# Seven products for part of the input stage of a fused attention and squared-ReLU kernel on one Trainium2 core

## The chip, the cores and the metric

The kernel runs on one core of one Trainium2 chip. The metric is the device time of one execution in microseconds; the kernel before has a median of 283.25 us over three runs (282.54 to 285.18). PE is TensorE, DVE VectorE, ACT ScalarE, POOL GpSimd, and SP the engine that issues most DMAs.

## The reference

Attention in chunks of 64 tokens is followed by a feed-forward layer with a squared ReLU. Scores and values stay within a chunk, so attention is small; the two products with w_in (512 x 2048) and w_out (2048 x 512) over 4608 tokens are nearly all of the arithmetic.

```python
scores = scale * np.matmul(q_c, k_c.transpose(0, 1, 2, 4, 3))   # chunks of 64 x 64
attn = np.exp(scores - max); attn = attn / (sum(attn) + 1e-09)
out = np.matmul(attn, v_c)
x = out.transpose(0, 2, 1, 3).reshape(B * S, H * D)             # 4608 x 512
h = np.maximum(x @ w_in, 0.0)
return (h * h @ w_out).astype(np.float32)
```

## The kernel before, in words

The 4608 tokens are 18 groups of 256, taken two at a time as 9 blocks (0 to 8) of 512 tokens. The groups of block 7 are put together from the last 64 tokens of each batch entry (`is_whole` is false for them); all others are contiguous.

Each block has an input stage and an output stage. The input stage (`ffn_in`, L455) takes the 16 tiles of 128 of d_ff one after the other, in the order 8 to 15, then 0 to 7: four matmuls of 512 columns into one PSUM bank (L480), a relu by ACT into `rl` (L471), and a square into `gT`, by ACT for tiles 10, 14 and 3 (L473) and else by DVE (L475). The output stage (`ffn_out`, L498; block 0 has a plain one) multiplies `gT` by w_out in seven products of quarters (Strassen's scheme in Winograd's manner of saving sums), 16 matmuls of 256 columns each (L533). Two chains of PSUM, n and m, hold sums that go on accumulating from product to product while ACT and DVE read partial sums from them (L580 to L616). DVE makes five differences of quarters of `gT` for it (`difference`, L510, recorded at L493).

The order of all work is written out by hand (`manual_schedule`): each engine runs its instructions in the order in which the program issues them. Both stages are generators that yield after each d_ff tile or each half of a product; a yield is a slot. Before the next slot the main loop (L700 to L780) issues at most one piece of a DMA load, then what the plan has for this slot, then stores that were put off (`late`). The plan of block j makes attention for block j+1: SC (scores, L355: 32 small matmuls and an exp by ACT, L385), AV (values, L387: two halves, each 16 small matmuls into a tile of `ps_att`, then on DVE a reciprocal, L408, and a multiplication, L409), and XT, a transposing DMA on SP that makes `xT` (L422); and for block j+2 casts of q and k on ACT (C, L333 and L340) and transposing DMAs (TD, L351). The usual slots are in L745: SC (4, 4), AV (7, 11), XT (10, 14), C (18, 22), TD (20, 24); other slots stand beside it for block 3 and for block 6, whose next block is not whole.

PSUM has 8 banks: four for `ps_ffn` and two tiles of two banks for `ps_att` (L64, L65). `rl` has three buffers, the input pool of q and k five. POOL casts weights and early q and k, in the first three blocks; after that it has nothing but the stores of the last block (L568).

Of the kernel before, what the change touches and what calls it, by code (L numbers as in the profile page):

```python
# [10 lines left out]
FP32 = mybir.dt.float32  # L11
BF16 = mybir.dt.bfloat16
AF = mybir.ActivationFunctionType
ALU = mybir.AluOpType
# [3 lines left out]
def kernel(  # L18
# [9 lines left out]
    nc = tc.nc  # L28

    B, H, S, D = q.shape  # L30
# [27 lines left out]
    const_pool = ctx.enter_context(tc.tile_pool(name="const", bufs=1))  # L58
    w_pool = ctx.enter_context(tc.tile_pool(name="w", bufs=1))
    wst_pool = ctx.enter_context(tc.tile_pool(name="wst", bufs=5))  # L60
    in_pool = ctx.enter_context(tc.tile_pool(name="qk", bufs=5))
    att_pool = ctx.enter_context(tc.tile_pool(name="att", bufs=3))
    ffn_pool = ctx.enter_context(tc.tile_pool(name="ffn", bufs=1))
    ps_ffn = ctx.enter_context(tc.tile_pool(name="ps_ffn", bufs=4, space=bass.MemoryType.PSUM))  # L64
    ps_att = ctx.enter_context(tc.tile_pool(name="ps_att", bufs=2, space=bass.MemoryType.PSUM))  # L65

    ctx.enter_context(tc.manual_schedule())

# [5 lines left out]
    w_in_bf = w_pool.tile([128, n_dt, d_ff], BF16, name="w_in_bf")  # L74
    w_out_bf = w_pool.tile([128, n_ft, d_model], BF16, name="w_out_bf")
    w_sum = w_pool.tile([128, 3, n_ft // 2, d_model // 2], BF16, name="w_sum")

    NV = 5
    NO = 2 * NV + 1
# [7 lines left out]
    qk = {}  # L87
# [299 lines left out]
    def values(g, tiles=(0, 1)):  # L387
        e = state["e", g]
        veb = v_even[g % NV].bitcast(BF16)
        vob = [v_odd[odd_tile[g, c] % NO].bitcast(BF16) for c in range(4)]  # L390
        if 0 in tiles:
            state["x", g] = att_pool.tile([128, 2, n_hp, 2, D], BF16, name="x", bufs=3)
        x = state["x", g]
        for t in tiles:
            ps = ps_att.tile([128, 2, 512], FP32, name="ps_att")
            for hp in range(n_hp):
                for a in range(2):
                    for p in range(2):
                        c = p ^ a
                        vb = vob[2 * t + p] if a else veb[:, t]  # L400
                        nc.tensor.matmul(  # L401
                            out=ps[64 * p:64 * p + 64, a, hp * (D + 1):(hp + 1) * (D + 1)],
                            lhsT=e[64 * c:64 * c + 64, a, hp, t, :],
                            rhs=vb[64 * c:64 * c + 64, hp, 1::2],
                            start=True, stop=True)
            o = ps[:, :, 0:n_hp * (D + 1)].rearrange("p a (h d) -> p a h d", d=D + 1)
            rec = att_pool.tile([128, 2, n_hp], FP32, name="rec", bufs=4)
            nc.vector.reciprocal(out=rec, in_=o[:, :, :, D])  # L408
            nc.vector.tensor_tensor(  # L409
                out=x[:, t].rearrange("p h a d -> p a h d"),  # L410
                in0=o[:, :, :, 0:D],
                in1=rec.to_broadcast([128, 2, n_hp, D]),
                op=ALU.mult)
# [21 lines left out]
    C, CQ, CK, TD = cast_qk, cast_q, cast_k, transpose_qk_dma  # L435
    SC, AV, XT = scores, values, transpose_x

    def TA(g):
        transpose_qk(g, ps_att, ps_att)

# [8 lines left out]

    gTs = {}  # L450
    LATE_STORES = {j: 26 if j == 2 else 20 for j in range(2, len(blocks) - 1)}
    late = []
    FT_ORDER = [*range(n_ft // 2, n_ft), *range(n_ft // 2)]

    def ffn_in(j, parts, begun={}):  # L455
        if j not in gTs:
            gTs[j] = ffn_pool.tile([128, n_ft, BT], BF16, name="gT")
        gT, xT = gTs[j], xTs[j]
        for u, (c, n, ft) in enumerate((c, n, ft) for c, n, fts in parts for ft in fts):
            h = begun.get(ft)  # L460
            if h is None:
                h = ps_ffn.tile([128, 512], FP32, name="ps_ffn")
            for dt in range(n_dt // 2 if ft in begun else 0, n_dt):
                ffn_in_step(h, xT, c, n, ft, dt)
            if j < 3:
                if n == 512 or u % 2 == 0:
                    rl_tile = ffn_pool.tile([128, 512], FP32, name="rl", bufs=3).bitcast(BF16)
                rl = rl_tile[:, u % 2 * 512:] if n < 512 else rl_tile
            else:
                rl = ffn_pool.tile([128, 512], FP32, name="rl", bufs=3)  # L470
            nc.scalar.activation(out=rl[:, 0:n], in_=h[:, 0:n], func=AF.Relu)  # L471
            if (n == 512 and ft in SQUARES_ON_ACT) or (n < 512 and ft in (12, 3)):
                nc.scalar.activation(out=gT[:, ft, c:c + n], in_=rl[:, 0:n], func=AF.Square)  # L473
            else:
                nc.vector.tensor_tensor(  # L475
                    out=gT[:, ft, c:c + n], in0=rl[:, 0:n], in1=rl[:, 0:n], op=ALU.mult)
            yield
# [14 lines left out]
    def add(engine, out, in0, in1, op=ALU.add):  # L492
        engine.tensor_tensor(out=out, in0=in0, in1=in1, op=op)  # L493
# [4 lines left out]
    def ffn_out(j):  # L498
# [28 lines left out]
        def product(name, a, b, first):  # L527
            if first:
                state["chain", name] = chain(name)
            outs = state["chain", name]  # L530
            for t in range(n_tt):
                for i in range(HF):
                    nc.tensor.matmul(  # L533
                        out=outs[t],
                        lhsT=a[:, i, t * 128:(t + 1) * 128],
                        rhs=b[:, i, :],
                        start=(first and i == 0 and (last or t == 0)), stop=(i == HF - 1),
                        skip_group_check=True)
                yield
# [69 lines left out]
        for ps, cols, t in parts("m"):  # L609
            add(nc.vector, c22[:, cols], ps, s[:, cols])  # L610
            store(nc.gpsimd, c22, 1, HD, t)
        yield from product("n", d7, b21_p_b22, False)
        c11 = o_tile()
        for ps, cols, t in parts("n"):
# [96 lines left out]
    for j, grps in enumerate(blocks):  # L711
# [4 lines left out]
        def at(slot, f, g):  # L716
            plan.setdefault(slot, []).append((f, g))
# [25 lines left out]
        else:  # L743
# [3 lines left out]
                slots.update({SC: (8, 8), AV: (10, 14), XT: (13, 17)})  # L747
                go_slots = [*range(6), *range(13, 32)]
            if not is_whole(nxt[0] if nxt else 0):
                slots.update({SC: (7, 7), AV: (9, 13), XT: (12, 16)})  # L750
            if j == 2:
                loads = itertools.chain(*map(v_pieces, nxt), loads)
                slots = {SC: (8, 10), AV: (12, 15), XT: (15, 18), C: (20, 23), TD: (22, 25)}
                go_slots = [*range(16), *range(25, 36)]
            for f in (SC, AV, XT):
                for i, g in enumerate(nxt):
                    at(slots[f][i], f, g)
            if j > 2 and far and is_whole(far[0]):
                for slot, f, i in ((16, CQ, 0), (18, CK, 0), (18, TD, 0), (18, CQ, 1),
                                   (19, CK, 1), (19, TD, 1)):  # L760
                    at(slot, f, far[i])
            else:
                for f in (C, TD):
                    for i, g in enumerate(far):
                        at(slots[f][i], f, g)
            phases = [ffn_in(j, [(0, BT, FT_ORDER)]), ffn_out(j)]
        slot = 0
        for phase in phases:
            for _ in phase:
# [43 lines left out]
```

## Time and profile before

| what | before |
|---|---|
| median of three runs | 283.25 us |
| the profiled execution's own time | 281.17 us |
| its span, first to last instruction | 279.4 us |
| input stage of block 4, 5, 6, 7, 8 | 15.79, 15.55, 15.81, 15.55, 13.81 us |
| output stage of block 4, 5, 6, 7 | 12.23, 12.23, 12.45, 12.23 us |
| POOL busy from block 3 to the end | 2.91 us |

The stages are read from the chain of waits: the chain runs along PE there, and each stage begins where its first matmul does. In the table of stretches each row is one stage: its length, then each engine's busy time with the number of instructions, the granted clock of TensorE, the DMA share. In the order of time, a row gives start, length, engine, line, operation, out<-in and shapes; a row with x2 or more is several instructions of one kind in a row, and what stands in brackets is the idle time ahead of it and what ended that. Matmul ends are modelled in the profile, so the mean spacing of many is a better measure of one than its own duration.

### The profile page before, as it was taken

Reading aid. Unit: us, or ns where it says so; the run is one execution under the profiler, and the core shown is the slowest. Engines: PE = TensorE matmul, PEld = TensorE weight load, DVE = VectorE, ACT = ScalarE, POOL = GpSimd, SP = SyncE. Lnnn points to the kernel's source line nnn. Section 1 sums busy time; section 2 is a strip of 40 time slices with the busy share of each in tenths; the row PEclk is TensorE's granted clock in tenths of the full one; section 3 lists DMA queues with packets and bytes.
Section 4 is the critical chain, followed back from the end, with each engine's and each line's share of the span. In section 5 each row is a group of like instructions: output and inputs, shape, how many; then the busy total and the mean of one; then the engine's idle time right before and its main releaser. Section 6 shows DMA issues by size and latency. Waiting matters only on the chain.

```text
span 279.4 us, 7179 instructions
## 1 busy us (share of the span) xinstructions
PE 269.2 (96%) x2960; PEld 176.2 (63%) x2963; DVE 186.5 (67%) x304; ACT 160.5 (57%) x269; POOL 35.8 (13%) x62
## 2 busy tenths in 40 slices
PE   6789999989999999999999999999999999999994
PEld 4544455878774487448744874487448744874584
DVE  1446414998943595579549954995579649955793
ACT  2537615885348862877197719762877197218710
POOL 2037844240171000000000000000000000000012
PEclk9999999999999999999999999999999999999998
DMA  7999999989999999979999999979699964141003
GB/s 236 220 345 358 364 332 240 326 212 194 255 207 244 238 213 191 258 183 198 218 245 260 187 184 298 191 158 185 196 238 208 212 199 40 39 109 44 0 21 131
DMA packets 144384, 57.09 MB, mean 204 GB/s; under 512 B 110624, under 2 KB 141600, under 8 KB 144352
## 3 DMA queue, kind: packets, MB, share of 16 engines
q1 hardware_dynamic: 143296, 53.62, 83.8%
q0 software_dynamic: 912, 2.88, 2.8%
q8 instruction: 23, 0.38, 0.6%
q10 hardware_dynamic: 144, 0.13, 0.1%
q14 instruction: 9, 0.07, 0.1%
HBM read 36.70 MB, written 9.44 MB: 165 GB/s over the span
## 4 chain that ended last, share of the span: by engine, by line
PE 80%; DVE 6%; SPq 4%; ACT 2%; DMA 2%; issue 2%; POOL 0%; DVEq 0%; ACTq 0%
PE ps_ffn L480 39%; PE ps_ffn L533 32%; PE ps_ffn L626 5%; SPq L236 3%; DMA w_st<-in_moe_w_in_dram 2%; DVE x L409 2%; DVE gT L475 2%; DVE w_st L493 2%; ACT rl L471 2%; PE ps_att L401 2%; PE ps_att L374 1%; ACT e L385 1%; SPq L227 1%; PE ps_att L428 1%; PE ps_att L190 1%
## 5 line engine op out<-in xcount | busy, mean ns | idle before, releaser
L480 PE MATMUL ps_ffn<-xT,w_in_bf 128*128 128x512 bf16 (+1 forms) x640 | 130.0, 358 | 0.7 <-POOL w_in_bf L165 0.7
L475 DVE TENSOR_TENSOR gT<-rl 128x512 bf16<-128x512 f32 (+2 forms) x132 | 74.2, 593 | 61.4 <-ACT rl L471 60.7
L471 ACT ACTIVATE rl<-ps_ffn 128x512 f32<-128x512 f32 (+2 forms) x160 | 85.7, 554 | 26.9 <-PE ps_ffn L480 23.3
L480 PEld LDWEIGHTS <-w_in_bf 128*128 128x128 bf16 x640 | 60.5, 98 | 58.2 <-POOL w_in_bf L165 2.2
L533 PEld LDWEIGHTS <-w_st 128*128 128x128 bf16 x640 | 62.0, 98 | 8.2 <-DVE w_st L493 0.9
L493 DVE TENSOR_TENSOR w_st<-gT 128x2048 bf16<-128x2048 bf16 x40 | 47.3, 1217 | 0.2
L533 PE MATMUL ps_ffn<-w_out_bf,w_st 128*128 128x256 bf16 x384 | 45.1, 273 | 0.1
L533 PE MATMUL ps_ffn<-w_sum,w_st 128*128 128x256 bf16 x256 | 29.6, 273 | 0.0
L616 ACT COPY o_sb<-ps_ffn 128x512 f32<-128x512 f32 (+1 forms) x8 | 4.5, 559 | 40.3 <-PE ps_ffn L533 40.3
L533 PEld LDWEIGHTS <-gT 128*128 128x128 bf16 x256 | 24.8, 98 | 4.4 <-DVE gT L475 0.2
L568 POOL DMA_DIRECT2D out_dram<-o_sb x4 | 2.2, 553 | 186.2 <-DVE o_sb L493 186.2
L409 DVE TENSOR_TENSOR x<-ps_att,rec 128x512 bf16<-128x512 f32 x32 | 22.1, 691 | 1.1
L385 ACT ACTIVATE e<-ps_att 128x1024 bf16<-128x1024 f32 x16 | 15.8, 1022 | 4.8 <-PE ps_att L374 4.8
L473 ACT ACTIVATE gT<-rl 128x512 bf16<-128x512 f32 (+2 forms) x28 | 16.8, 599 | 0.9
L533 PE MATMUL ps_ffn<-w_out_bf,gT 128*128 128x256 bf16 x128 | 15.3, 273 | 0.0
L533 PE MATMUL ps_ffn<-w_sum,gT 128*128 128x256 bf16 x128 | 15.3, 273 | 0.0
L626 PE MATMUL ps_ffn<-w_out_bf,gT 128*128 128x512 bf16 x61 | 14.2, 379 | 0.3 <-issue 0.2
L165 POOL CAST w_in_bf<-w_st 128x1024 bf16<-128x1024 f32 (+1 forms) x9 | 9.0, 1001 | 17.9 <-DMA w_st<-in_moe_w_in_dram 17.9
L340 ACT CAST qkb<-k_sb 128x1024 bf16<-128x1024 f32 x10 | 10.5, 1047 | 1.2 <-DMA k_sb<-in_k_dram 1.2
L333 ACT CAST qkb<-q_sb 128x1024 bf16<-128x1024 f32 x10 | 10.4, 1044 | 0.0
L626 PEld LDWEIGHTS <-gT 128*128 128x128 bf16 x64 | 6.0, 98 | 7.0
L401 PEld LDWEIGHTS <-e 64*64 64x64 bf16 x512 | 5.8, 107 | 6.3 <-DVE x L409 2.1
(63 smaller groups left out, 157.1 us busy)
## 6 DMA issues: line engine op xcount, KB each, us to landing
q_sb<-in_q_dram SPq DMA_DIRECT2D x16, 512.0 KB, 6.2
k_sb<-in_k_dram SPq DMA_DIRECT2D x24, 256.0 KB, 5.8
out_dram<-o_sb SPq DMA_DIRECT2D x20, 256.0 KB, 3.7
w_st<-in_moe_w_in_dram SPq DMA_DIRECT2D x8, 512.0 KB, 6.8
w_st<-in_moe_w_out_dram SPq DMA_DIRECT2D x8, 512.0 KB, 6.1
ve_sb<-in_v_dram SPq DMA_DIRECT2D x28, 128.0 KB, 3.5
vo_sb<-in_v_dram SPq DMA_DIRECT2D x21, 128.0 KB, 3.0
out_dram<-o_sb POOLq DMA_DIRECT2D x9, 256.0 KB, 5.5
```

Source lines behind the costliest of these rows:

```text
L333: copy(out=qkb[:, 0].rearrange("p (i h d) -> p i h d", i=2, h=H), in_=qk[g][0].rearrange("p t h d -> p (t h d)").rearrange("p (h i d) -> p ...
L340: copy(out=state["qkb", g][:, 1], in_=qk[g][1].rearrange("p t h d -> p (t h d)"))
L385: nc.scalar.activation(out=e_out, in_=s_in, func=AF.Exp, scale=scale)
L401: nc.tensor.matmul(out=ps[64 * p:64 * p + 64, a, hp * (D + 1):(hp + 1) * (D + 1)], lhsT=e[64 * c:64 * c + 64, a, hp, t, :], rhs=vb[64 * c: ...
L409: nc.vector.tensor_tensor(out=x[:, t].rearrange("p h a d -> p a h d"), in0=o[:, :, :, 0:D], in1=rec.to_broadcast([128, 2, n_hp, D]), op=AL ...
L471: nc.scalar.activation(out=rl[:, 0:n], in_=h[:, 0:n], func=AF.Relu)
L473: nc.scalar.activation(out=gT[:, ft, c:c + n], in_=rl[:, 0:n], func=AF.Square)
L475: nc.vector.tensor_tensor(out=gT[:, ft, c:c + n], in0=rl[:, 0:n], in1=rl[:, 0:n], op=ALU.mult)
L480: nc.tensor.matmul(out=h[:, 0:n], lhsT=w_in_bf[:, dt, ft * 128:(ft + 1) * 128], rhs=xT[:, c // 128:(c + n) // 128, dt, :], start=(dt == 0) ...
L493: engine.tensor_tensor(out=out, in0=in0, in1=in1, op=op)
L533: nc.tensor.matmul(out=outs[t], lhsT=a[:, i, t * 128:(t + 1) * 128], rhs=b[:, i, :], start=(first and i == 0 and (last or t == 0)), stop=( ...
L626: nc.tensor.matmul(out=o_ps[tt], lhsT=gT[:, ft, tt * 128:(tt + 1) * 128], rhs=w_out_bf[:, ft, :], start=(ft == 0), stop=(ft == n_ft - 1))
```

## The change

For four d_ff tiles (12 to 15) of blocks 4, 5 and 7, and for eight (12 to 15 and 4 to 7) of block 8, the input stage is done by seven products as well: 512 model columns and 512 tokens and four tiles are halved each, and 7 x 4 matmuls of 256 columns take the place of 16 of 512. This is called a unit. It needs

- five differences of quarters of w_in, by POOL: `w_differences`, at slot 2 of block 3 for tiles 12 to 15, and at slot 0 of block 6 for tiles 4 to 7 (into buffers of the input pool);
- three sums of quarters of xT, by DVE, near the end of the output stage of the block before (`x_sums`);
- two PSUM banks, `ps_unit`: from block 4 on `ps_att` has one tile in place of two. Unit b of block 8 takes two banks of `ps_ffn`;
- seven additions and copies that read the chains, and relu with square of the four quarters: three by one DVE operation each (`scalar_tensor_tensor`: max with 0, then times itself), put off to given slots (`LATER`), the fourth by ACT's relu and a square on POOL.

In these blocks the squares of the plain tiles are dealt out anew (`SQUARE_BY`: five on POOL and four on ACT, or four and four in block 8). The units' products alternate with plain tiles (`ORDER`), so an input stage has 19 or 22 slots. Attention has slots of its own there, with the halves of AV apart; C, TD and the late stores move by three slots. Block 6 has new slots for SC, AV and XT. `rl` has five buffers, the input pool four.

The core of the diff, with "..." where lines are left out:

```diff
-    in_pool = ctx.enter_context(tc.tile_pool(name="qk", bufs=5))
+    in_pool = ctx.enter_context(tc.tile_pool(name="qk", bufs=4))
-    ps_att = ctx.enter_context(tc.tile_pool(name="ps_att", bufs=2, space=bass.MemoryType.PSUM))
+    ps_att, ps_unit = psum_pool("ps_att", 2), None
...
+    UNITS = {4: (12,), 5: (12,), 7: (12,), 8: (12, 4)}
+    for j in UNITS:
+        if j in LATE_STORES:
+            LATE_STORES[j] += 3
...
+        for d, (x, y) in zip(out, pairs):
+            add(nc.gpsimd, d, quarter(f0, *x), quarter(f0, *y), ALU.subtract)
...
+        add(nc.vector, by_dt, xT[:, :, 0:2], xT[:, :, 2:4])
+        add(nc.vector, cross, xT[:, 0:2, 0:2], xT[:, 2:4, 2:4], ALU.subtract)
+        add(nc.vector, by_t, xT[:, 0:2], xT[:, 2:4])
...
+    def unit(j, f0, n, m, kept, later):
...
+        product(n, quarter(f0, 1, 1), by_dt[:, 0:2], True)
+        n1 = kept("n1")
+        nc.scalar.copy(out=n1, in_=n)
+        yield
+        product(m, quarter(f0, 0, 0), by_dt[:, 2:4], True)
+        w = kept("nm")
+        add(nc.vector, w, m, n1)
+        yield
+        product(n, dif[0], xT[:, 2:4, 2:4], False)
+        n2 = kept("n2")
+        nc.scalar.copy(out=n2, in_=n)
+        yield
+        product(m, dif[1], xT[:, 0:2, 0:2], False)
+        c21 = rl_tile_fp32()
+        add(nc.vector, c21, w, m, ALU.subtract)
+        c12 = rl_tile_fp32()
+        add(nc.gpsimd, c12, w, n2, ALU.subtract)
+        relu_squared(c21, 1, 0)
+        relu_squared(c12, 0, 1)
+        yield
+        product(n, dif[2], cross, False)
+        s = kept("n1")
+        add(nc.vector, s, n, n2, ALU.subtract)
+        yield
+        product(m, dif[3], by_t[:, :, 0:2], False)
+        c22 = rl_tile_fp32()
+        add(nc.vector, c22, m, s)
+        relu_squared(c22, 1, 1)
+        yield
+        product(n, dif[4], by_t[:, :, 2:4], False)
+        c11 = rl_tile_fp32()
+        nc.scalar.activation(out=c11, in_=n, func=AF.Relu)
+        add(nc.gpsimd, place_of(0, 0), both(c11), both(c11), ALU.mult)
+        yield
+
+    ORDER = {1: (8, 9, 10, "a", 11, "a", 0, "a", 1, "a", 2, "a", 3, "a", 4, "a", 5, 6, 7),
+             2: (8, 9, "a", 10, "a", 11, "a", "b", "a", 0, "b", "a", "b", "a", 1, "b", "a", "b",
+                 2, "b", "b", 3)}
+    SQUARE_BY = {1: {9: "A", 1: "A", 4: "A", 6: "A", 10: "P", 0: "P", 2: "P", 3: "P", 5: "P"},
+                 2: {9: "A", 11: "A", 0: "A", 3: "A", 8: "P", 10: "P", 1: "P", 2: "P"}}
+    LATER = {1: (5, 10, 13, 15), 2: (9, 12, 14, 16, 18, 21)}
...
+        if j + 1 in UNITS:
+            state["x_sums"] = x_sums(j + 1)
         yield from product("n", d7, b21_p_b22, False)
...
             if not is_whole(nxt[0] if nxt else 0):
-                slots.update({SC: (7, 7), AV: (9, 13), XT: (12, 16)})
+                slots.update({SC: (6, 8), AV: (10, 14), XT: (12, 16)})
...
+            if j in UNITS:
+                late_by = 3
+                go_slots = range(35)
+                for i, g in enumerate(nxt):
+                    for slot, f in zip(((4, 9, 11, 13), (7, 14, 16, 19))[i], (SC, AV0, AV1, XT)):
+                        at(slot, f, g)
+                nxt = []
+            if j == 3:
+                at(2, lambda _: w_differences(UNITS[4][0], [w_dif[:, n] for n in range(5)]), None)
+            if j == 4:
+                att_psum.close()
+                ps_att, ps_unit = psum_pool("ps_att", 1), psum_pool("ps_unit", 2)
+            if j == 6:
+                at(0, w_differences_again, None)
```

`relu_squared` puts its DVE operation on the list `later`; `ffn_in_units` walks `ORDER`, issuing either a unit's next product or a plain tile, and takes one operation off that list at each index in `LATER`. `AV0` and `AV1` are `values` for its first and its second half.

## The prediction

> **What bounds the kernel now.** I read the page's busy times and chain first, then a table of stretches (one row for the input stage and one for the output stage of a block), then the chain of waits for blocks 4 and 5, then the order of time on DVE and POOL at the places that the change touches.
>
> ```profile
> PE 269.2 (96%) x2960; PEld 176.2 (63%) x2963; DVE 186.5 (67%) x304; ACT 160.5 (57%) x269; POOL 35.8 (13%) x62
> PE 80%; DVE 6%; SPq 4%; ACT 2%; DMA 2%; issue 2%; POOL 0%; DVEq 0%; ACTq 0%
> ```
>
> TensorE (PE) is the bound: 96% busy and 80% of the chain. So an edit is worth what it does to PE: matmul time that goes, and pauses that come.
>
> ```profile
> 138.00:153.79 15.79, 15.74 (x195) 7.42 (x193) 10.07 (x19) 12.71 (x21) 0.00 (x0) 1.00 1.01 251
> 193.80:209.61 15.81, 15.75 (x194) 7.47 (x193) 9.50 (x17) 12.63 (x21) 0.00 (x0) 1.00 0.87 225
> 222.06:237.61 15.55, 15.55 (x194) 7.36 (x193) 9.84 (x19) 12.64 (x21) 0.00 (x0) 1.00 0.61 128
> 249.84:263.65 13.81, 13.81 (x67) 6.30 (x65) 7.47 (x12) 10.98 (x19) 0.00 (x0) 1.00 0.19 45
> ```
>
> These are the input stages of blocks 4, 6, 7 and 8 (stretch, length, then busy time of PE, weight loads, DVE, ACT, POOL, the granted clock, the DMA share and GB/s). PE fills each one; the clock is 1.00. Block 8 has no attention in it: 64 matmuls of 512 columns in 13.81 us, 215.8 ns each.
>
> ```profile
> 166.02 4.32 PE ps_ffn L480 x20
> 170.34 0.64 PE ps_att L374 x64
> 170.98 2.69 PE ps_ffn L480 x12
> 173.67 0.39 PE ps_att L401 x32
> 174.06 3.56 PE ps_ffn L480 x16
> 177.62 0.39 PE ps_att L401 x32
> 178.01 3.56 PE ps_ffn L480 x16
> 181.57 12.23 PE ps_ffn L533 x112
> ```
>
> This is the chain in block 5 (start, length, what). 112 matmuls of 256 columns take 12.23 us, 109.2 ns each. Sixteen matmuls of 512 with a visit to attention before or in them take 3.56, not 3.45: a visit costs some 0.1 us beside its own matmuls.
>
> **Part 1, the products.** Four d_ff tiles are 16 matmuls of 512 (16 x 215.8 = 3.453 us); by seven products they are 28 of 256 (28 x 109.2 = 3.058). Each unit saves 0.395 us, five units 1.98 us, all on PE. That is the whole gain, 0.7%.
>
> **Part 2, visits.** In blocks 4, 5 and 7 attention is now visited six times (two SC, four half AV) instead of three: 3 x 3 x 0.1 = +0.9 us; block 6 gets its two SC apart: +0.1.
>
> **Part 3, one ps_att buffer, block 6.** From block 4 on ps_att has one buffer in place of two. Blocks 4, 5 and 7 call the halves of AV in slots apart; block 6 still calls AV whole (slots 10 and 14). There the second half's matmuls cannot start until DVE has read the first half's (rec, then x), and all of PE's queue stands behind them. The same work before:
>
> ```profile
> 203.97 1.29 DVE L475 TENSOR_TENSOR gT<-rl 128x512 bf16<-128x512 f32 x2 [1.62 <-ACT rl L471]
> 205.18 0.20 DVE L408 RECIPROCAL rec<-ps_att 128x8 f32<-128x8 f32 x1
> 205.41 0.69 DVE L409 TENSOR_TENSOR x<-ps_att,rec 128x512 bf16<-128x512 f32 x1
> 206.02 0.20 DVE L408 RECIPROCAL rec<-ps_att 128x8 f32<-128x8 f32 x1
> ```
>
> DVE takes the square of the slot's own d_ff tile first, and that square waits for ACT's relu. The first AV's first half left PE at about 203.7 and its x ended at 206.10: 2.4 us. For the second AV (207.6 to 209.80) it is 2.2 us. With two buffers nobody waited for this. Worked from the parts: 0.25 to the relu, relu 0.60, square 0.61, rec 0.24, x 0.69 are 2.4 after the tile's last matmul, less the 0.3 of the first half itself: 2.1. Bounds: 1.2 (rec and x alone after 0.25) and 2.4 each. Nothing excludes the squares, which the code puts in front: I take 2.25 each, +4.5 us. Against it, what block 6 loses now over block 7's 15.55 and over 12.23 (0.26 in the input stage, 0.22 in the output stage, both from DVE and ACT being behind) goes, since PE's pause lets them catch up: -0.5. Net +4.0.
>
> **Part 4, one buffer in blocks 4, 5, 7.** Between the two halves of an AV, PE has one tile of 512 (0.86) and one product (0.44): 1.30 us. DVE needs 0.25 + 0.24 + 0.69 = 1.18 if it is free. The margin is 0.1, and in front of rec stand a c21 addition (slot 9) or a relu-square (slot 13) of 0.6, the latter perhaps held by POOL (part 5). There are two such places in a block, and two more where SC or AV waits for an exp (0.25 and 1.03, with some 1.3 to 1.75 of PE work for cover): waits from 0 to some 0.6 at the first two, little at the others. Bounds 0.1 and 1.2 per block, I take 0.4, three blocks +1.2. The DVE load itself falls there (10 squares fewer at 0.60, 7 new operations), so its share is no evidence of cover; the order in the queue decides.
>
> **Part 5, POOL.** No elementwise operation of two inputs on POOL is in the trace. Nearest rows: a cast of 512 takes 0.61, one of 1024 takes 1.04, twice the first 1.23. Two inputs of 512 read as many elements as a cast of 1024, so I take 1.04, bounds 0.61 and 1.23. A unit block gives POOL 7 of them, 7.3 us of 15: not a bound. But POOL and DVE hinder each other:
>
> ```profile
> 25.00 1.04 POOL L165 CAST w_in_bf<-w_st 128x1024 bf16<-128x1024 f32 x1 [0.22 <-DMA w_st<-in_moe_w_in_dram]
> ```
>
> ```profile
> 23.46 0.42 DVE L475 TENSOR_TENSOR gT<-rl 128x512 bf16<-128x512 bf16 x1 [1.49 <-ACT rl L471]
> ...
> 25.25 1.41 DVE L475 TENSOR_TENSOR gT<-rl 128x512 bf16<-128x512 bf16 x2 [0.19 <-ACT rl L471]
> ```
>
> A square that takes 0.42 alone started 0.25 after a cast on POOL and, with a second one behind it, lasted to 26.66: the first can have done next to nothing before the cast ended at 26.04. [...]
>
> **Part 6, block 8.** Its order leaves DVE late. After unit a's fourth product PE has four tiles of 512 (3.46) and nine products (3.93), 7.4 us. DVE has 13 operations of 0.605: 7.9 us. The last product of unit b needs the tenth of them, at best 0.25 + 6.05 + 0.08 = 6.4 after, where PE would be there at 6.1; and in between DVE idles for c12 and for w. Six of these have two SBUF inputs, among six POOL operations of 1.04, so a collision costs up to 1 us and some half on the mean. Bounds 0.3 (no collision) and 2.2 (three or four in front of that product); I take +1.4, waits before unit b's sixth and seventh products.
>
> **What I cost at nothing, and its cover.** The three sums of x (1024, 512, 1024 columns, by the rows 0.42 for 512 and 1.22 for 2048 some 0.7 + 0.4 + 0.7) run after DVE's last addition of an output stage, which ended at 165.00 in block 4; their first reader stands three tiles into the next block (166.02 + 2.59 = 168.6), 1.8 us of cover; without it PE would wait by the excess, in three or four blocks. They need xT, whose second transpose (SP, L422) went out at 161.50 and takes 3.5 to land: 165.0. It moves from slot 14 to 19 behind up to five more loads; block 4 has none left by then, block 5 has five (5 x 0.65 = 3.2 us; it went out at 181.90 there, so it lands at 188.6, before 192), block 7 has no loads. The stores and the qk transposes move by 3 slots as the stage does. The weight differences (5 x 1.04 on POOL in blocks 3 and 6) hold squares back at most by one POOL operation each; rl has five buffers now. The input pool's four buffers always hold tiles cast a block earlier. Laying out PSUM anew waits for x of block 3 (127.2), 10 us before.
>
> **Sum.** -1.98 + 0.9 + 0.1 + 4.0 + 1.2 + 1.4 = +5.6. The profiled execution's own time is 281.17 (span 279.4 and 1.8 around it), so 286.8 there. The median of the runs, 283.25, lies 2.1 above it; on it the changed kernel comes to 288.9, which I predict.
>
> **Rivals.**
> A (not slower): block 6's wait is short, DVE comes to rec at once, and collisions on POOL are rare. Waits of 1.2 each (2.4 - 0.5), 0.2 a block in part 4, 0.3 in block 8: -1.98 + 1.0 + 1.9 + 0.6 + 0.3 = +1.8, 285.1. For it: PE's pause in slot 10 also leaves ACT free. Against it: the square in front of rec is in program order. It decides where block 6's two pauses are under 1.7 us each with these other terms (sum +2.8). Truly faster by over 1% would need -2.8, and parts 1 and 3 offer at most -2.5: only a cost that is negative where I see none.
> B: POOL sets the pace. At 1.23 each and every collision hit: part 4 at 1.2 a block, part 6 at 2.2: -1.98 + 1.0 + 4.0 + 3.6 + 2.2 = +8.8, 292.1. For it: the row above; against: DVE's load falls.
> C: xT comes too late for its sums. If SP's loads hold the second transpose 2 us more than counted, unit a waits 1 us in three blocks: +8.6, 291.9. For it: 5 loads moved ahead; against: it landed 8 us early in block 5.
>
> **Chances.** Forecast 0.60, A 0.17 (most of it within 1%), B 0.12, C 0.05, and 0.06 that I misread a term and it is faster. Measurement tells about 1% (2.8 us): faster below 280.4, slower above 286.1. Faster 0.05, same 0.15, slower 0.80. Range 284.9 to 292.3, which takes in A and B; the forecast's own range is 286.5 to 291.
>
> **What would show it.** Block 6's input stage at about 20.1 us with two pauses before matmuls of L401's line on x; blocks 4, 5, 7 at about 15.9; block 8 at about 14.4 with pauses before products; output stages at 12.23; POOL operations of 512 at 1.04. Wrong, if block 6 stays under 17.5 us, if POOL's operations take over 1.3 us, or if DVE waits for xT at the end of an output stage.

## The result, and the profile after

| | before | after |
|---|---|---|
| median | 282.72 us (281.04 to 285.18, 6 runs) | 293.86 us (291.67 to 296.3, 6 runs) |
| the profiled execution's own time, span | 281.17, 279.4 us | 294.93, 293.1 us |

The ratio is 1.0412, with a 95% interval of 1.0373 to 1.0452; the medians are 11.1 us apart. The ratio leaves out the slowest run after, 296.3, which lies over 1.5% above the fastest. The prediction was +5.6 us and 288.9, with a range up to 292.3. The direction was right, the size was half of what came, and the range missed by 1.6 us.

The page of the changed kernel, its span, busy times and the shares of the chain:

```profile
span 293.1 us, 7338 instructions
PE 273.8 (93%) x3023; PEld 183.9 (63%) x3023; DVE 199.1 (68%) x308; ACT 159.4 (54%) x268; POOL 86.4 (29%) x101
PE 24%; DVE 7%; issue 2%; ACT 1%; DVEq 0%
```

The chain's shares add up to 34% here, against 96% before: it was followed back over a third of the span only, so the two rows of shares can't be set against each other. The busy row can: PE's share fell from 96% to 93%, and its idle time grew from about 10 to 19 us. PE is still what bounds the kernel, but now something makes it wait. Where, the table of stretches tells. In order: input stage of block 4, output stage of block 5, input and output stage of block 6, input stages of blocks 7 and 8 (columns as before):

```profile
140.19:156.41 16.22, 15.93 (x206) 8.46 (x204) 10.05 (x19) 12.01 (x21) 7.57 (x7) 1.00 1.04 251
184.87:199.48 14.61, 12.71 (x113) 10.86 (x112) 12.79 (x11) 6.03 (x8) 9.39 (x6) 1.00 0.69 153
199.48:220.35 20.87, 16.80 (x194) 7.65 (x192) 11.36 (x20) 12.54 (x21) 0.00 (x0) 0.97 0.97 229
220.35:233.68 13.33, 13.33 (x114) 11.51 (x113) 10.67 (x14) 5.54 (x7) 0.00 (x0) 0.92 0.71 156
233.68:249.90 16.22, 15.93 (x207) 8.45 (x205) 10.04 (x19) 12.02 (x21) 7.57 (x7) 1.00 0.20 51
262.12:277.32 15.20, 13.34 (x90) 8.59 (x88) 10.63 (x15) 9.72 (x17) 8.56 (x7) 1.00 0.18 45
```

Set beside the table before, stage by stage:

| stage | before | after | forecast of the difference | measured |
|---|---|---|---|---|
| input of blocks 4, 5, 7 | 15.78, 15.55, 15.55 | 16.22, 16.22, 16.22 | +0.9 together | +1.8 |
| output of block 5 | 12.23 | 14.62 | 0 | +2.4 |
| input and output of block 6 | 15.81, 12.45 | 20.87, 13.32 | +4.1 together | +5.9 |
| input of block 8 | 13.81 | 15.20 | +0.6 | +1.4 |
| other stages from block 4 on | | | 0 | 0 |

The sum is +11.5, which is what the medians say (+11.1). Block 4 begins 2.3 us later in this profile (140.19 against 137.85), in the blocks that the change all but leaves alone; experiments e1, e2 and e4 show that it can begin as early as before.

**Block 6, input stage.** The order of time on DVE around the first pause, then the chain on PE, then from the list of waits (in total, how often, the longest):

```profile
210.31 1.29 DVE L639 TENSOR_TENSOR gT<-rl 128x512 bf16<-128x512 f32 x2 [0.59 <-ACT rl L635]
211.52 0.20 DVE L416 RECIPROCAL rec<-ps_att 128x8 f32<-128x8 f32 x1
211.75 0.69 DVE L417 TENSOR_TENSOR x<-ps_att,rec 128x512 bf16<-128x512 f32 x1
212.88 0.21 DVE L416 RECIPROCAL rec<-ps_att 128x8 f32<-128x8 f32 x1 [0.43 <-PE ps_att L409]
```

```profile
211.75 0.70 DVE x L417
212.45 0.04 issue
212.50 0.32 PE ps_att L409 x15
212.82 3.57 PE ps_ffn L644 x16
217.89 0.70 DVE x L417
218.60 0.04 issue
218.64 0.33 PE ps_att L409 x14
```

```profile
PE ps_att L409 <- DVE x L417: 4.0, 2, 2.0
```

The second half of AV (L409) starts 0.04 us after the first half's `x` has ended, twice, and PE does nothing from the end of the first half on: 2.0 us each in the list of waits. The square still stands in front of `rec`, as before; what is new is that DVE's second `rec` now waits for PE. Each engine waits for the other in turn over the single buffer.

**The clock.** In block 6 the granted clock is 0.97 and 0.92 where it was 1.00. Three stretches of 2 us around the second pause:

```profile
217.00:219.00 2.00, 0.36 (x17) 0.31 (x18) 1.50 (x3) 0.02 (x1) 0.00 (x0) 1.00 0.99 222
219.00:221.00 2.00, 2.00 (x8) 0.85 (x8) 0.90 (x2) 0.41 (x1) 0.00 (x0) 0.54 1.22 213
221.00:223.00 2.00, 2.00 (x13) 1.49 (x12) 1.74 (x2) 1.12 (x2) 0.00 (x0) 0.60 0.96 112
```

After the second pause the clock is at half from 219.18 to 222.59 us, 3.41 us, and matmuls of 512 columns follow one another by 427 ns, not 216. That costs half of 3.41, 1.7 us.

**Block 5, output stage.** POOL, and then DVE, in order of time:

```profile
182.77 2.54 POOL L657 TENSOR_TENSOR gT<-rl 128x512 bf16<-128x512 f32 x2 [1.35 <-ACT rl L564]
185.27 6.90 POOL L657 TENSOR_TENSOR q_sb<-w_in_bf 128x512 bf16<-128x512 bf16 x4
192.13 2.13 POOL L657 TENSOR_TENSOR k_sb<-w_in_bf 128x512 bf16<-128x512 bf16 x1
```

```profile
187.07 4.08 DVE L657 TENSOR_TENSOR w_st<-gT 128x2048 bf16<-128x2048 bf16 x2
191.08 0.68 DVE L657 TENSOR_TENSOR nm<-ps_ffn,n 128x512 f32<-128x512 f32 x1
191.68 3.66 DVE L657 TENSOR_TENSOR w_st<-gT 128x2048 bf16<-128x2048 bf16 x2
195.86 1.21 DVE L657 TENSOR_TENSOR w_st<-gT 128x2048 bf16<-128x2048 bf16 x1
```

The five differences of w_in that the code issues at slot 0 of block 6 run here, a stage earlier: POOL has nothing ahead of them and their inputs lie ready, so it goes on. DVE makes its differences of `gT` at the same time. Pairs of them take 4.08 and 3.66 us, where the last one, which starts after POOL is through, takes 1.21. PE's products wait for them: 12.71 us busy of 14.61.

**Block 8.** The two places on PE, and one DVE and one POOL row:

```profile
274.35 0.60 PE L515 MATMUL ps_ffn<-w_st,q_sb 128*128 128x256 bf16 x4 [0.78 <-DVE rl L657]
276.03 0.60 PE L515 MATMUL ps_ffn<-w_st,k_sb 128*128 128x256 bf16 x4 [1.08 <-DVE q_sb L657]
```

```profile
268.68 1.65 DVE L529 SCALAR_TENSOR_TENSOR gT<-rl 128x512 bf16<-128x512 f32 x1
```

```profile
263.92 1.04 POOL L657 TENSOR_TENSOR gT<-rl 128x512 bf16<-128x512 f32 x1 [13.58 <-ACT rl L603]
268.52 1.27 POOL L657 TENSOR_TENSOR rl<-nm,n 128x512 f32<-128x512 f32 x1 [1.00 <-ACT n L543]
```

Unit b's sixth and seventh products are late, by 0.94 and 1.25 us in spacing of starts (the brackets show less, since matmul ends are modelled). A relu-square on DVE that takes 0.68 alone began 0.16 after a POOL operation and ended 0.54 after it: it got next to nothing done before POOL was through. A square on POOL takes 1.04 us where DVE is idle (263.92). The subtraction c12, with results in float32, takes 1.27 also in block 4 (at 147.73), where no relu-square runs beside it, so its 1.27 here is no sign that it was held.

### The profile page after: what moved, and what is told of

Same layout as the page of the kernel before. It is cut to its first block, busy times and chain, and to the rows that moved or that the text cites. A ratio compares the mean times of both kernels' runs of the same rounds, so it can differ in the third digit from the quotient of the medians.

```text
span 293.1 us, 7338 instructions
## 1 busy us (share of the span) xinstructions
PE 273.8 (93%) x3023; PEld 183.9 (63%) x3023; DVE 199.1 (68%) x308; ACT 159.4 (54%) x268; POOL 86.4 (29%) x101
## 5 line engine op out<-in xcount | busy, mean ns | idle before, releaser
L644 PE MATMUL ps_ffn<-xT,w_in_bf 128*128 128x512 bf16 (+1 forms) x560 | 116.9, 356 | 1.7 <-POOL w_in_bf L172 1.7
L644 PEld LDWEIGHTS <-w_in_bf 128*128 128x128 bf16 x560 | 52.5, 98 | 45.2 <-POOL w_in_bf L172 2.9
L657 POOL TENSOR_TENSOR gT<-rl 128x512 bf16<-128x512 f32 x24 | 27.8, 1167 | 140.9 <-ACT rl L603 136.8
L639 DVE TENSOR_TENSOR gT<-rl 128x256 bf16<-128x256 bf16 (+2 forms) x80 | 44.9, 592 | 33.6 <-ACT rl L635 32.7
L635 ACT ACTIVATE rl<-ps_ffn 128x512 bf16<-128x512 f32 (+2 forms) x96 | 48.2, 525 | 21.7 <-PE ps_ffn L644 21.0
L603 ACT ACTIVATE rl<-ps_ffn 128x512 f32<-128x512 f32 x44 | 26.3, 597 | 14.3 <-PE ps_ffn L644 13.4
L697 PEld LDWEIGHTS <-gT 128*128 128x128 bf16 x256 | 25.5, 100 | 5.1 <-issue 0.6
L409 PEld LDWEIGHTS <-e 64*64 64x64 bf16 x512 | 6.3, 107 | 12.8 <-DVE x L417 8.4
L529 DVE SCALAR_TENSOR_TENSOR gT<-rl 128x512 bf16<-128x512 f32 x15 | 13.6, 906 | 0.1
L409 PE MATMUL ps_att<-ve_sb,e 64*64 64x65 bf16 x256 | 9.0, 198 | 4.9 <-DVE x L417 4.9
L657 DVE TENSOR_TENSOR gT<-rl 128x512 bf16<-128x512 f32 x9 | 6.5, 722 | 8.3 <-ACT rl L603 8.3
```

The costliest lines, as they stand in the source:

```text
L409: nc.tensor.matmul(out=ps[64 * p:64 * p + 64, a, hp * (D + 1):(hp + 1) * (D + 1)], lhsT=e[64 * c:64 * c + 64, a, hp, t, :], rhs=vb[64 * c: ...
L529: later.append(lambda: nc.vector.scalar_tensor_tensor(out=place_of(i, jj), in0=both(x), scalar=0.0, in1=both(x), op0=ALU.max, op1=ALU.mult))
L603: nc.scalar.activation(out=rl, in_=h, func=AF.Relu)
L639: nc.vector.tensor_tensor(out=gT[:, ft, c:c + n], in0=rl[:, 0:n], in1=rl[:, 0:n], op=ALU.mult)
L644: nc.tensor.matmul(out=h[:, 0:n], lhsT=w_in_bf[:, dt, ft * 128:(ft + 1) * 128], rhs=xT[:, c // 128:(c + n) // 128, dt, :], start=(dt == 0) ...
L697: nc.tensor.matmul(out=outs[t], lhsT=a[:, i, t * 128:(t + 1) * 128], rhs=b[:, i, :], start=(first and i == 0 and (last or t == 0)), stop=( ...
```

## The experiments

**Theory after the result.** Four things add up: (1) the single `ps_att` buffer in block 6, with the clock drop that follows its pauses; (2) the second set of weight differences, which runs early and holds DVE up; (3) a visit to attention that costs about 0.2 us, not 0.1; (4) POOL and DVE holding each other up in block 8. The main rivals: that `rl` and input buffers slowed the front; that block 6 is slow by its slots; that POOL's work costs nothing and DVE's queue alone makes the waits.

### e1: block 6 with the halves of AV apart

The changed kernel, with the slots of block 6 set so that other work lies between the halves:

```diff
             if j == 6:
                 at(0, w_differences_again, None)
+                for i, g in enumerate(nxt):
+                    for slot, f in zip(((4, 8, 11, 12), (6, 13, 16, 17))[i], (SC, AV0, AV1, XT)):
+                        at(slot, f, g)
+                nxt = []
```

> Theory (one PSUM buffer makes two pauses of 2.0 to 2.1 us in block 6, and the second of them lets the clock fall to half for 3.4 us, 1.7 us more): with the halves of AV in slots three apart the input stage of block 6 falls from 20.87 to about 16.0, the output stage after it from 13.32 to 12.3, and the whole by 5.5 to 6 us against the changed kernel. Rival 1 (only the pauses count, the clock drop has another cause): 4.1 us less, and the granted clock still dips. Rival 2 (the pauses only show a lag of DVE that PE would meet anyway): under 2 us less.

287.49 us, ratio 1.023 (1.021 to 1.025), against 1.0412 of the changed kernel. The input stage of block 6:

```profile
196.95:212.93 15.98, 15.93 (x178) 7.25 (x176) 9.40 (x17) 12.65 (x21) 0.00 (x0) 1.00 0.93 231
```

15.98 in place of 20.87, the output stage 12.59 in place of 13.32, the clock 1.00 throughout. PE is busy for all but 0.05 us. The single buffer with these slots, and what it brought with it, was worth 5.6 us by stages. e1 moves the slots of SC too, and no run gives block 6 its second buffer back; that PE's two pauses are waits for the buffer is read from the rows above.

### e2: no second set of weight differences

Left out: the differences for tiles 4 to 7; block 8's unit b multiplies by those of 12 to 15.

```diff
-                at(0, w_differences_again, None)
+                difs[UNITS[8][1]] = difs[UNITS[8][0]]
```

> Leaves out the five differences of w_in for tiles 4 to 7 (unit b of block 8 multiplies by those of tiles 12 to 15). Theory (POOL runs them as soon as it is idle, in block 5's output stage, and there they hold back DVE's differences of gT): that stage falls from 14.62 to 12.2 to 12.4, all other stages stay, 2.3 us less in all. Rival (that stage is long since DVE comes late out of the input stage of block 5, by its squares): it stays above 14, and the whole the same within 0.5 us.

290.19 us, ratio 1.0316 (1.0259 to 1.0373). Output stage of block 5, input stage of block 6:

```profile
182.58:194.81 12.23, 12.23 (x113) 10.96 (x112) 9.72 (x11) 6.04 (x8) 0.44 (x1) 1.00 0.64 142
194.81:216.79 21.98, 17.91 (x194) 7.96 (x192) 11.28 (x20) 12.73 (x21) 0.00 (x0) 0.92 1.04 231
```

The output stage is back at 12.23 us, and DVE's busy time in it went from 12.79 to 9.72 for the same 11 operations: the 2.4 us were POOL's doing. In this execution the clock fell after the first pause, so all of its cost lies in the input stage (21.98) and the output stage of block 6 took 12.23.

### e3: matmuls in the pauses

Sixteen matmuls of no use in block 6, into `ps_unit`, ahead of each second half of AV; if the clock falls because PE stands still, it should no longer fall, and the pause itself stays.

```diff
         for t in tiles:
+            if t == 1 and 0 in tiles and place[g][0] == 7:
+                keep_busy(16, ps_unit.tile([128, 512], FP32, name="ps_unit"))
```

> Adds 16 idle matmuls of 256 columns (1.75 us) into an unused bank between the two halves of AV in block 6, once for each group, so that PE is busy while it would wait. Theory (it is the idle time of PE that takes the clock down): the clock stays at 1.00 through block 6, the pauses stay, and the whole is 1.7 us shorter though more is computed. Rival (the clock falls by its own time or by something else): the same dip, and a time that is the same or up to 0.4 us longer.

291.01 us, ratio 1.0358 (1.0329 to 1.0387). Input stage of block 6:

```profile
197.48:217.77 20.29, 19.93 (x226) 10.52 (x224) 11.19 (x20) 12.54 (x21) 0.00 (x0) 1.00 1.01 212
```

20.29 and 12.23, clock 1.00: 1.7 us less than the changed kernel in these two stages. But the fall doesn't come in every execution. In six profiled executions with both pauses unfilled it came in four (after, e2, e12, e13) and not in two (e5 and e11, which also took 20.29 and 12.23). The traces show what set the six apart. In each of the four the fall comes a whole number of stretches of 3.413 us after the clock first rose to full speed (62, 59, 60 and 60 of them, to within 0.01), and the clock stays down for one such stretch. The length is read off the clock's own record: in the changed kernel it is at full speed for 211.63 us from 7.55 us on, at half for 3.413 and at full speed again for 71.68, and the first and the last are 62.0 and 21.0 times 3.413; in the kernel before it is at full speed for 273.07 us, 80.0 times. Each trace cut into stretches of 3.413 us from that first rise:

| execution | idle time of PE in the emptiest stretch of the two stages | clock |
|---|---|---|
| after | 2.00 us (215.76 to 219.18) | falls at 219.18 |
| e2 | 2.02 us (204.71 to 208.13) | falls at 208.13 |
| e12 | 2.02 us (207.32 to 210.73) | falls at 210.73 |
| e13 | 2.02 us (207.93 to 211.34) | falls at 211.34 |
| e5 | 1.53 us (211.76 to 215.17) | stays |
| e11 | 1.65 us (214.19 to 217.60) | stays |

The rows of the changed kernel and of e11:

```profile
215.76:219.18 3.42, 1.42 (x37) 0.69 (x36) 2.86 (x6) 0.99 (x2) 0.00 (x0) 1.00 0.88 197
```

```profile
214.19:217.60 3.41, 1.76 (x23) 0.70 (x21) 2.50 (x5) 1.87 (x4) 0.00 (x0) 1.00 0.94 215
```

A pause of 2.0 us that lay whole in one stretch was followed by a fall at the end of that stretch. A pause that the border between two stretches cut was not: in the changed kernel's first pause 1.87 us lay in one stretch, and the clock stayed. In block 6, then, 1.87 us of idle time in a stretch left the clock alone and 2.00 us did not. At the start of the kernel, among other kinds of matmul, it isn't the same: in the profiled executions of e6 and e7 (mean clock 0.988 and 0.994) the clock fell there after stretches with 1.4 us of idle time. Filled pauses leave no stretch of block 6 with over 0.5 us idle, and e3's clock stays at 1.00.

The mean clock of the runs without a profile agrees, but weakly. One fall in some 290 us makes it 1 - 1.7 / 290 = 0.994. With the pauses unfilled, 13 of the 18 runs that count had 0.994 or less; with them filled none of four did (0.999 to 1.0), and in e1 and e6, which have no pauses in block 6, one of eight (e6's profiled execution, which fell at the start). But 15 of 43 runs of the kernel before, timed beside the experiments, had it too. The ratio's interval touches that of the changed kernel. What a fall costs is plain: the two stages take 34.2 us in all four executions that have one (20.87 + 13.32, 21.98 + 12.23, 21.97 + 12.23, 21.94 + 12.23) and 32.5 without.

### e4: the kernel before, with the new buffers

```diff
-    in_pool = ctx.enter_context(tc.tile_pool(name="qk", bufs=5))
+    in_pool = ctx.enter_context(tc.tile_pool(name="qk", bufs=4))
...
-                rl = ffn_pool.tile([128, 512], FP32, name="rl", bufs=3)
+                rl = ffn_pool.tile([128, 512], FP32, name="rl", bufs=5)
```

> The kernel before, with four buffers in place of five in the input pool and five in place of three for rl. Theory (blocks 0 to 2 took 2.3 us longer in the changed kernel by chance of how the weights' DMAs ran): the same as before within 0.5 us, block 4 begins near 137.9. Rival (fewer input buffers hold loads back, or the new addresses slow DMAs): 2 us longer, block 4 begins near 140.

281.62 us, ratio 1.0012 (0.9988 to 1.0037); block 4 began at 138.41. The buffers cost nothing that shows, and the changed kernel can come without the 2.3 us at its front: in e1 and e2 block 4 began at 137.66 and 137.91. What they are in that one profile stays open.

### e5: POOL's squares read nothing

Left out: POOL's squares of the plain tiles, in all unit blocks; POOL fills the tile with a constant.

```diff
-                    add(nc.gpsimd, gT[:, ft], rl, rl, ALU.mult)
+                    nc.gpsimd.memset(gT[:, ft], 0.5)
```

> Leaves out the squares that POOL makes for plain tiles in blocks 4, 5, 7 and 8 and writes a constant in their place, so that POOL reads nothing for them; its c12 and c11 operations stay. Theory (POOL's reads hold back DVE's operations with two SBUF inputs, and so the sums that unit b's sixth and seventh product wait for): of the 2.2 us that PE loses in block 8 some 1.5 go, the stage falls from 15.20 to about 13.7, and blocks 4, 5 and 7 fall from 16.22 by the 0.3 to 0.4 of the last AV's wait. Rival (DVE's own queue of 13 operations in 7.4 us is the cause): block 8 stays above 14.8 and the other blocks at 16.2.

291.11 us, ratio 1.0336 (1.0296 to 1.0376). Input stages of blocks 4 and 8:

```profile
138.08:153.94 15.86, 15.86 (x206) 8.46 (x204) 9.62 (x19) 11.94 (x21) 3.69 (x5) 1.00 1.02 254
257.09:272.54 15.45, 13.34 (x91) 8.58 (x88) 10.85 (x16) 9.73 (x17) 4.93 (x5) 1.00 0.18 44
```

Blocks 4, 5 and 7 went from 16.22 to 15.86, and PE is never idle there: the 0.36 us was one wait, at the second half of the second AV, and it came from DVE being held by POOL. In the changed kernel's block 5 that wait is this row:

```profile
182.87 0.22 PE L409 MATMUL ps_att<-ve_sb,e 64*64 64x65 bf16 x2 [0.29 <-DVE x L417]
```

Block 8 missed its expectation: 15.45, not shorter but longer than 15.20. The two POOL operations of each unit that still read (c12 and the last square) only moved: they now fell on DVE's relu-squares, which took 1.61 and 1.44 us. Taking away some of the collisions shifted the rest; e12 takes all of them away.

### e6: the second differences tied to block 6

e1, and a copy of one column on POOL that reads the first square of block 6, so that the differences behind it can't start in block 5.

```diff
-                at(0, w_differences_again, None)
+                def tied(_):
+                    nc.gpsimd.tensor_copy(out=ident_f32[:, 0:1], in_=gTs[6][:, FT_ORDER[0], 0:1])
+                    w_differences_again(None)
+                at(0, tied, None)
```

> The halves of AV apart in block 6 as before, and the second set of differences made to wait, by a copy of one column on POOL that reads the first square of block 6, so that POOL makes them in the input stage of block 6. Theory (they cost only where they meet DVE's five long differences): block 5's output stage falls from 14.62 to 12.23, block 6's input stage grows by at most 0.5 over 15.98, and the whole is 1.9 to 2.4 us under the run with the halves apart alone. Rival (they cost wherever DVE works): block 6 grows by 1.5 or more and the whole stays within 0.9.

285.98 us, ratio 1.0148 (1.0114 to 1.0182), against 1.023 of e1. Output stage of block 5, input stage of block 6:

```profile
184.67:196.89 12.22, 12.22 (x113) 10.96 (x112) 9.72 (x11) 6.03 (x8) 0.44 (x1) 1.00 0.74 152
196.89:213.02 16.13, 16.01 (x178) 7.23 (x176) 13.16 (x17) 12.74 (x21) 7.54 (x6) 1.00 1.03 242
```

The same five differences cost 2.4 us in block 5's output stage and 0.15 in block 6's input stage (16.13 for e1's 15.98). DVE loses as much in the one as in the other (9.40 us busy in e1's block 6, 13.16 here, for 17 operations each), but in the input stage PE rarely waits for it. The two were timed beside different runs of the kernel before (medians 282.1 and 281.2), so the ratios compare them: 1.023 less 1.0148 is 2.3 us, as the stages say (the bare medians are 1.5 apart). The profiled execution of e6 shows the same trap once more: the first set (slot 2 of block 3) ran in block 2, whose input stage took 17.40 us, against 15.78 before. In e11 and e13 too that set began 1.8 us into the stage, and it took 17.41; where the set began 2.65 us in or later it took 15.78 to 16.34. So it goes with the moment at which POOL comes free, and it differs between executions; no run puts it to the test.

### e7: a unit in block 8 alone

```diff
-    UNITS = {4: (12,), 5: (12,), 7: (12,), 8: (12, 4)}
+    UNITS = {8: (12,)}
```

with one set of differences, block 6's old slots, and PSUM laid out anew at block 8.

> One unit, in block 8 alone, where no attention is; PSUM laid out anew only there, blocks 4 to 7 as in the kernel before. Theory (the products save what they save, 0.395 us, and all losses come from the visits, the one buffer and POOL's and DVE's queues): the input stage of block 8 is 13.4 to 13.5, the other stages those of before, and the whole 0.3 to 0.5 us under the kernel before, which is within what a measurement can tell. Rival (a unit costs more than it saves even alone): 13.8 or more there and no gain.

280.62 us (12 runs), ratio 0.9972 (0.9952 to 0.9992). Input stage of block 8:

```profile
249.83:263.25 13.42, 13.42 (x79) 7.44 (x77) 7.42 (x11) 10.13 (x19) 6.50 (x7) 1.00 0.20 49
```

13.42 for 13.81: 0.39 us, the whole of what part 1 gives a unit (0.395), with PE never idle. The products are worth what their matmuls say. On the medians of the runs it is 1.5 us under the kernel before and by the ratio 0.8 (0.2 to 1.4); the stages show 0.39 of that.

### e8: the kernel before, with the halves apart

In blocks 4 to 7 of the kernel before, two buffers kept, the halves of AV are put one slot apart: two more visits per block, and nothing else.

```diff
-            for f in (SC, AV, XT):
+            if j >= 4:
+                for i, g in enumerate(nxt):
+                    at(slots[AV][i], AV0, g)
+                    at(slots[AV][i] + 1, AV1, g)
+            for f in (SC, XT) if j >= 4 else (SC, AV, XT):
```

> The kernel before, two buffers as it has, with the halves of AV one slot apart in blocks 4 to 7: two visits of PE to attention more in each. Theory (a visit costs PE 0.2 us, 0.1 on the way in and 0.1 on the way out): the input stages of blocks 4 to 7 are 0.4 us longer, 15.95 in place of 15.55, and the whole 1.6 us longer. Rival (0.1 a visit, as predicted): 15.75 and 0.8 us.

283.22 us, ratio 1.0032 (0.9998 to 1.0065). Input stage of block 5:

```profile
167.77:183.78 16.01, 16.01 (x194) 7.30 (x192) 10.14 (x19) 12.72 (x21) 0.00 (x0) 1.00 0.76 188
```

16.01 for 15.55, PE never idle: 0.23 us per visit. The whole grew by 0.9 us by the ratio, for 1.6 expected, with an interval that reaches just below zero, so the price rests on the stage. The chain shows one AV with its halves apart, and the tiles behind it:

```profile
175.58 0.26 PE ps_att L401 x16
175.84 0.97 PE ps_ffn L486 x4
176.81 0.26 PE ps_att L401 x16
177.07 2.69 PE ps_ffn L486 x12
```

Before, the same work was 0.39 for 32 small matmuls and 3.56 for 16 of 512. The prediction's 0.1 was read from the second alone, and there it is right: 0.97 + 2.69 is 0.10 more. The other 0.13 lies in the rows of the small matmuls, which take 0.26 for 16, and not half of 0.39.

### e11 to e13: block 8 by itself

In these three the transposing DMAs are plain copies of the same tiles, so the transposition of `xT` and `qkT` is left out. e11 is the changed kernel with that alone, and the one to compare with. e12 leaves out also all of POOL's work in block 8 (constants are written in its place); e13 puts the second unit's relu-squares later.

```diff
+        if j == 8:
+            nc.gpsimd.memset(c12, 0.5)
+        else:
+            add(nc.gpsimd, c12, w, n2, ALU.subtract)
...
-    LATER = {1: (5, 10, 13, 15), 2: (9, 12, 14, 16, 18, 21)}
+    LATER = {1: (5, 10, 13, 15), 2: (9, 13, 17, 19, 20, 21)}
```

(The first hunk is e12's, with the same for the two squares; the second is e13's.)

> The control for the two runs that follow: the changed kernel with its transposing DMAs made plain copies of the same bytes, which leaves out the transposition of q, k and x. Every theory: block 8, which issues none of these DMAs and has its xT long before, keeps its input stage of 15.2 us and its two waits of 2.2 us in sum.

> With the same plain copies as the control. Leaves out everything that POOL computes in block 8 (four squares, c12 of both units, c11 squared of both) and writes constants instead, so that POOL reads nothing there; DVE's 13 operations stay in their order. Theory (exclusion by POOL's reads makes most of the 2.2 us that PE loses in block 8): no operation of DVE takes over 0.75 us there, and the input stage falls from 15.2 to 13.3 to 13.7. Rival (DVE's queue alone): 14.8 or more.

> With the same plain copies as the control. Only the indices at which block 8 takes its put-off relu-squares are changed (9, 13, 17, 19, 20, 21 in place of 9, 12, 14, 16, 18, 21), so that fewer of them stand on DVE in front of the sums which unit b's sixth and seventh product wait for. Theory (the order in DVE's queue decides what PE loses): PE's losses in block 8 fall from 2.2 to about 1 us, the stage to 13.9 to 14.3. Rival (DVE is simply full there): the losses move to other products or to the output stage, and the two stages together keep 27.5 us or more.

e11 and e12 ran once each (292.54 and 291.45 us), so they speak by their stages alone; e13 took 294.37, ratio 1.0394 (1.0289 to 1.0499). The input stage of block 8 in e11, e12 and e13, with the output stage behind it for e13:

```profile
259.76:274.96 15.20, 13.34 (x90) 8.58 (x88) 10.63 (x15) 9.73 (x17) 8.56 (x7) 1.00 0.19 44
```

```profile
259.92:273.62 13.70, 13.18 (x91) 8.62 (x89) 9.10 (x16) 9.73 (x17) 2.92 (x6) 1.00 0.21 49
```

```profile
274.84:288.56 13.72, 12.78 (x113) 10.68 (x111) 12.56 (x19) 3.48 (x8) 5.16 (x7) 1.00 0.07 27
```

e11 repeats the changed kernel (15.20). In e12 the stage takes 13.70, and the same relu-square that took 1.65 takes 0.69:

```profile
266.48 0.69 DVE L529 SCALAR_TENSOR_TENSOR gT<-rl 128x512 bf16<-128x512 f32 x1
```

So 1.5 of the 2.2 us of waits came from POOL's operations that read, and 0.7, before the last product, from DVE's queue alone. The prediction's bound without collisions was 0.3; a relu-square that reads the sum just ahead of it begins 0.72 after that sum, not 0.6, and there are three of these in the way. In e13 the input stage took 14.12 and the output stage 13.72 where it had 12.39: 27.84 together, against 27.59. Putting DVE's work off only moved the waits into the next stage.

## Why the prediction was wrong

**What bounds the kernel, and part 1: right.** PE sets the time; e7 shows the gain per unit at 0.39 (0.395 forecast).

**Part 2, visits: mis-sized.** 0.1 us was taken, 0.23 measured (e8). It counted what a visit adds to the tiles beside it and left out what it adds to its own matmuls. Nine more visits in blocks 4, 5 and 7 are +2.1, not +0.9. A block there adds up: 15.55 - 0.395 + 3 x 0.23 = 15.85, and 15.86 is what it takes when nobody waits (e5).

**Part 3, one buffer in block 6: right.** Two pauses of 2.0, at the places named, for 2.25 each; the sum of parts in the prediction, 2.1, was nearer. (The 203.7 that it reads as the end of the first AV's first half lies near the end of the second half; the first was through by 203.44.) Without the clock drop the two stages take 20.29 and 12.23, +4.3 over before, for +4.1 with the one visit. The output stage's recovery was right also (12.45 to 12.23).

**The clock: missed.** No step had it. The prediction read "the clock is 1.00" and did not ask whether the pauses it was forecasting would change that. It cost 1.7 us in this profile. The runs show the clock at half for 3.41 us (matmuls of 512 columns 427 ns apart, not 216) after a stretch of 3.41 us with 2.0 us idle and 1.4 us busy, four times. Whether it fell went by where the pause lay in the stretch: four falls in six executions (the table at e3).

**Part 4, one buffer in blocks 4, 5 and 7: right.** 0.36 a block for 0.4, from DVE held by POOL at the second AV (e5).

**Part 5, POOL: its price, and that it and DVE hinder each other, right.** A square takes 1.04 us, as taken from the cast of 1024; c12 takes 1.27. The squares' mean of 1.167 comes from those that start while DVE is in a relu-square: alone two in a row take 2.04 (e7), behind DVE 2.54 (182.77 above). On DVE it was the operations with both inputs in SBUF that were held, those that part 6 counts: relu-squares took up to 1.65 us (0.68 alone), two differences of `gT` 4.08 (2.36 in block 4). The 18 float32 additions with an operand in PSUM that ran beside an operation of POOL in the changed kernel took 0.68 to 0.69, the 30 others 0.67 to 0.69.

**Part 6, block 8: mis-sized.** Waits of 2.2, the upper bound, before the two products named, for 1.4. Collisions gave 1.5, and the queue without them 0.7 for the 0.3 of the lower bound (e12). The prediction took half a collision on the mean; the kernel's order is the same in each execution, and the collisions fell on the same operations each time (15.20, 15.21 and 15.20 us in the changed kernel, e1 and e11), so there was no mean to take.

**"What I cost at nothing": the step that failed.** "The weight differences (5 x 1.04 on POOL in blocks 3 and 6) hold squares back at most by one POOL operation each." It asked what the differences would delay on POOL, not what they would take from DVE, and it took the slot for the time. Nothing held them, so the second set ran in block 5's output stage, and there DVE's differences of 1.2 us feed PE directly: +2.4 us (e2). Part 5 had rows of the same kind, squares on DVE held behind a cast on POOL. The first set, too, cost block 2 some 1.6 us in three profiled executions (e6, e11, e13), though not in the changed kernel's own.

**The sum.** From +5.6: weight differences +2.4, the clock +1.7, visits +1.2, block 8 +0.8; and -0.2 for block 4, which took 15.79 before where block 5 took 15.55, so it grew by less. That is +11.5, what the stages show. Rival B (POOL sets the pace, 292.1) came nearest, by another road: POOL never was the bound, its collisions were. C fell: DVE's sums of xT cost nothing, and the output stages of blocks 3, 4 and 7 stayed at 12.50, 12.23 and 12.23.

Left open: how much idle time in a stretch the clock bears in general, and when POOL reaches the first set of differences.

## What to carry to other kernels

Work given to an idle engine can start long before the slot where it is written (here at 185.27 us, 14 us ahead of the block in whose slot 0 it stands); ask what runs on the other engines at that earlier time, and tie it to something later if it would hold them up. A single buffer between PE and DVE turned DVE's queue into two pauses of PE of 2.0 us here, so give each half other work to lie behind, as e1 does (15.98 us for 20.87). A rearrangement that saves 0.4 us a time must be priced with what it makes PE do besides: here the three added visits of a block took 0.7.

## What the runs showed of the hardware

- In block 6 the granted clock fell to half at whole multiples of 3.413 us after its first rise, for 3.41 us, when a pause of PE of 2.0 us lay whole in the stretch before (the changed kernel, e2, e12, e13); where a border cut the pauses, with at most 1.65 us idle in a stretch, it stayed (e5, e11).
- DVE's operations with both inputs in SBUF and POOL's operations that read held each other up where they met: DVE's relu-square took 0.68 to 1.65 us and two differences of 2048 columns 2.36 to 4.08 (the changed kernel), two squares on POOL 2.04 (e7) to 2.54 (the changed kernel), a weight difference there 1.1 (five in 5.58, e11) to 2.13 (the changed kernel). DVE's float32 additions with an operand in PSUM took 0.67 to 0.69 with and without POOL beside them. A fill on POOL, which reads nothing, took 0.5 us, and with fills alone no relu-square took over 0.69 (e12).
- A visit of PE to the small matmuls of attention cost 0.23 us beyond their work, 0.13 in their own rows and 0.10 in those behind (e8).
